# Reordering a fused attention and SwiGLU kernel on one core: scores two units at a time, rest products bank by bank, single steps unsplit

## The chip, the cores and the metric

The kernel runs on one core of one Trainium2 chip. Its engines run side by side, each through its own instructions in the order in which the kernel issues them: PE (TensorE, matmuls and weight loads), ACT (ScalarE), DVE (VectorE), POOL (GpSimd) and SP, which here only starts transfers. The metric is the device time of one execution in microseconds (us); less is better. Three runs of the kernel before gave 430.53, 430.70 and 430.71 us, so the median is 430.70 us.

## The reference

The inputs q, k, v have shape 8 x 12 x 448 x 64 (batch, head, sequence, head dimension). What is computed is attention, and then a SwiGLU block on its output as 3584 tokens of 768 values, with 1536 hidden values:

```
scores = (q @ k.T) / sqrt(64)
attn   = softmax(scores)
x      = (attn @ v), heads side by side     # 3584 x 768
g      = x @ w_gate
out    = ((g / (1 + exp(-g))) * (x @ w_val)) @ w_out
```

## The kernel before

**Units and pairs.** Two heads make a pair; there are 48 pairs, six per batch. Pairs 0 to 11 cut the 448 keys into four chunks of 112. One pair and one chunk is a unit. From pair 12 on (QUAD) a pair has three chunks of 128 keys, and the 64 keys left over, its rest, share one tile with the rest of the neighbouring pair.

For a unit, `qk` (lines 353 to 367; `qk_quad`, lines 324 to 351, from pair 12) does one score matmul per head on PE, into one tile of the pool `ps_s`, and one exponential of both heads on ACT. The score matmuls contract over 64 rows, one head on each half of the array. `ps_s` has three tiles of two banks each, handed out in turn: whoever takes a tile waits until the tile three places earlier has been read. `ps_f` has two tiles of one bank.

The product with the values follows later. In batch 0 it is `pv_chunk` (lines 377 to 411, called a piece here): eight matmuls into the pair's `ps_f` bank, and at the pair's fourth chunk a reciprocal and a multiplication on DVE. `copy_v` (line 216) brings the values into place on DVE; `prep(pr)` gives `turn` (lines 293 to 303), 18 transposes of queries and keys on PE into a tile of `ps_s`, with a copy on DVE; `turn_x` (lines 475 to 493) turns a finished pair on PE, three matmuls, and copies it on DVE into X, which the SwiGLU block reads.

From pair 12 on the product is `pv_open` (two banks, one per head), `pv_rest` (lines 439 to 442: for each of four query blocks j, for each head hx, one matmul with the 64 leftover keys; the two heads use different halves of the array's rows and different banks), `pv_pieces` (24 matmuls on full rows) and `pv_close` (DVE).

**The first stage.** Batch 0 runs ahead of the SwiGLU work. The loop at lines 1129 to 1151 goes through 24 units, one at a time: the unit's scores, then what stands behind it (a turn, loads, a value copy at the units in CAT, a `turn_x` at those in XAT, zero to two pieces). What is left of the pieces follows in the main loop's first visit (lines 1219 to 1223), after the scores of two more units and `turn_x(4)`. Then the first SwiGLU step begins; its `late` call is `turn_x(5)`, in the middle of its gate product.

**The main loop.** `plan` pairs score chunks with value products, two or three units a visit. Each visit's amount of SwiGLU work is written out in FIRST_STEPS and VISITS (lines 977 to 986). A Step (lines 546 to 624) is a gate product (six matmuls, 384 or 512 wide), a tanh on ACT, a value product and two DVE operations (lines 610 and 616). A split step does its value product in two halves, each closed by itself on DVE: the first half into the spare bank of the gate's `ps_s` tile, the second into a `ps_f` bank. `run_pair` splits the second of its steps; `run_single` (lines 1043 to 1049) is used where a visit has one step. In the trace it occurs three times, at 268.2, 279.3 and 290.4 us, each with 384 columns. In the last part the SwiGLU products are done in another form (Unit, `out_group`), which the change does not touch.

The order is the program's: every engine takes its instructions in the order of these calls.

Of the kernel before, what the change touches and what calls it, by code (L numbers as in the profile page):

```python
# [23 lines left out]
FIRST = 6  # L24
# [40 lines left out]
def kernel(  # L65
# [15 lines left out]
    NC = S // P  # L81
# [9 lines left out]
    KR = MQ // 128  # L91
# [68 lines left out]
    def dummy(n, w=4):  # L160
        wp = ps_f.tile([128, 512], FP32, tag="f", name="wp")
        for _ in range(n):
            nc.tensor.matmul(wp[:, 0 : w * 128], lhsT=warm[:], rhs=warm4[:, 0:w], start=True, stop=True)
# [52 lines left out]
    def copy_v(pr):  # L216
        m = 128 if pr >= QUAD else P
        nc.vector.tensor_copy(Vts[pr % NV][0:m, :, :, 0:D], vraw[0:m, pr % VS])
# [105 lines left out]
    def qk_quad(pr, c):  # L324
        s = ps_s.tile([128, 2, 512], FP32, tag="s", name="s")
        if c < KR:
            t = qkT[pr]
            for hx in range(2):
                nc.tensor.matmul(  # L329
                    s[:, hx, 0:S],  # L330
                    lhsT=t[ts(hx, 64), ts(c + low(pr, hx), 128)],
                    rhs=t[ts(hx, 64), ds(NC * 128, S)],
                    start=True,
                    stop=True,
                )
        else:
            for hx in range(2):
                for p in (pr, pr + 1):
                    lo = low(p, hx)
                    t = qkT[p]  # L340
                    nc.tensor.matmul(  # L341
                        s[ts(1 - lo, 64), hx, 0:S],
                        lhsT=t[ts(hx, 64), ds(0 if lo else KR * 128 + 64, 64)],
                        rhs=t[ts(hx, 64), ds(NC * 128, S)],
                        start=True,
                        stop=True,
                    )
        e = e_new(pr, c)
        nc.scalar.activation(  # L349
            e[:, 0 : 2 * S].rearrange("p (h q) -> p h q", h=2), s[:, :, 0:S], AF.Exp, scale=sm_scale  # L350
        )

    def qk(pr, c):
        if pr >= QUAD:
            return qk_quad(pr, c)
        t = qkT[pr]
        s = ps_s.tile([128, 2, 512], FP32, tag="s")
        for hx in range(2):
            nc.tensor.matmul(  # L359
                s[:, hx, 0:S],  # L360
                lhsT=t[ts(hx, 64), c * P : c * P + 128],
                rhs=t[ts(hx, 64), ds(S + (1 - hx) * D, S)],
                start=True,
                stop=True,
            )
        e = Es[pr % NE][:, ds(c * EB, 16)].rearrange("p (h b) x -> p h (b x)", h=2)
        nc.scalar.activation(e[:, :, 0:S], s[0:P, :, 0:S], AF.Exp, scale=sm_scale)  # L367
# [9 lines left out]
    def pv_chunk(pr, c):  # L377
        if c == 0:
            accs[pr] = ps_f.tile([128, 512], FP32, tag="f", name="acc")
        e = Es[pr % NE]  # L380
        vo = Vts[pr % NV][0:P]
        a7 = accs[pr][:, 0 : 7 * (D + 1)].rearrange("p (s d) -> p s d", s=7)
        for j in range(3):
            for hx in range(2):
                nc.tensor.matmul(  # L385
                    a7[:, 2 * j + hx],
                    lhsT=e[:, ds(c * EB + 9 * hx + 2 * j, 2)].rearrange("p b x -> p (b x)"),
                    rhs=vo[:, hx, c, 0 : D + 1],
                    start=c + j + hx == 0,
                    stop=False,  # L390
                )
        for hx in range(2):
            nc.tensor.matmul(
                a7[:, 6],
                lhsT=e[:, ds(c * EB + 6 + hx, 2)].rearrange("p b x -> p (b x)"),
                rhs=vo[:, hx, c, 0 : D + 1],
                start=False,
                stop=c == NC - 1 and hx == 1,
            )
        if c < NC - 1:  # L400
            return
        r = attp.tile([128, 8], FP32, tag="R8", bufs=2, name="R")
        xt = Xts[pr % NX]
        nc.vector.reciprocal(r[:, 0:7], a7[:, :, D])
        n = 7
        nc.vector.tensor_tensor(
            xt[:, 0:n],
            a7[:, 0:n, 0:D],
            r[:, 0:n].unsqueeze(2).to_broadcast([128, n, D]),
            ALU.mult,  # L410
        )

    def pv_mm(pr, hx, c, j, acc, first, last):
        lo = low(pr, hx)
        if c < KR:
            rows, e, col = slice(0, 128), eslot[pr, c][0], c + lo
        else:
            rows, col = (slice(0, 64), 0) if lo else (slice(64, 128), KR)
            e = eslot[pr - pr % 2, RU][0]
        nc.tensor.matmul(  # L420
            acc[:, ts(j, D + 1)],
            lhsT=e[rows, ds(hx * S + j * 128, 128)],
            rhs=Vts[pr % NV][rows, hx, col, 0 : D + 1],
            start=first,
            stop=last,
        )
# [10 lines left out]
            pv_mm(pr, hx, c, j, accs[pr][hx], False, c == KR - 1 and j == KR)  # L437

    def pv_rest(pr):
        for j in range(KR + 1):  # L440
            for hx in range(2):
                pv_mm(pr, hx, RU, j, accs[pr][hx], j == 0, False)

    def pv_close(pr, hx):
# [30 lines left out]
    def turn_x(pr):  # L475
        b, hp = divmod(pr, NHP)
        kk, bb = divmod(b, NB)
        if kk not in X:
            X[kk] = xp.tile([128, NCB, NB * S], FP16, tag="X", name="X")
        dst = X[kk][:, hp, ts(bb, S)]  # L480
        xt = Xts[pr % NX]
        if pr < XPE:
            tp = accs[pr] if pr < FIRST else ps_f.tile([128, 512], FP32, tag="f", name="xtp")
            for j in range(3):
                nc.tensor.matmul(
                    tp[:, ts(j, 128)],
                    lhsT=xt[:, 2 * j : 2 * j + 2].rearrange("p h d -> p (h d)"),
                    rhs=ident[:],
                    start=True,
                    stop=True,  # L490
                )
            nc.vector.tensor_copy(dst[:, 0:MQ], tp[:, 0:MQ])
            return
        nc.sync.dma_start_transpose(
            dst[:, 0:MQ].rearrange("p (j q) -> p j q", j=KR),
            xt[:, 0 : 2 * KR].rearrange("p j d -> p (j d)"),
        )
        nc.sync.dma_start_transpose(
            dst[:, MQ:S].rearrange("p (j q) -> p j q", j=1),
            xt[0:D, 2 * KR : 2 * KR + 2].rearrange("p h d -> p (h d)"),  # L500
        )
# [18 lines left out]
    gate_small = [False]  # L520
# [363 lines left out]
    with tc.manual_schedule():  # L884
# [33 lines left out]
        def emit(item):  # L918
            if item[0] == "qk":
                load_qk16(*item[1:])  # L920
            elif item[0] == "V":
                load_v(item[1] * GP, GP)
            else:
                load_w(*item)
# [86 lines left out]
        def add_sum(n=1):  # L1011
            for _ in range(n):
                if sums:
                    sums.pop(0)()
# [27 lines left out]

        def run_single():
            step = fvq.pop(0)
            step.split = step.alone = not gate_small[0]
            step.gate()
            step.value(0)
            step.finish()
            add_sum()
# [69 lines left out]
        def share(total, at, n):  # L1119
            return (at + 1) * total // n - at * total // n  # L1120

        XAT = (10, 14, 17, 21)
        CAT = (3, 7, 9, 13, 17, 21)
        pieces = [(p, c) for p in range(FIRST) for c in range(NC)]

        def piece():
            pv_chunk(*pieces.pop(0))

        for u in range(FIRST * NC):
            pr, c = divmod(u, NC)  # L1130
            qk(pr, c)
            if u == 1:
                dummy(1)
                turn()
                dummy(1)
            elif u == 3:
                dummy(2)
            elif u == 4:
                prep(2)()
            elif u >= 6 and c == 2:  # L1140
                prep(pr + 2)()
            if c == 1:
                for w in wq.pop(pr, []):
                    emit(w)
            if u in CAT:
                copy_v(CAT.index(u))
            if u in XAT:
                turn_x(XAT.index(u))
            for _ in range(2 if c == 3 else int(c != 2 or u > 12)):
                if u >= 4 and pieces[0][0] * NC + pieces[0][1] <= u - 3:  # L1150
                    piece()

        queue = []
        units = [divmod(x, NC) for x in range(QUAD * NC)]
# [11 lines left out]
        while g < last or queue:  # L1166
            n = 2 if g < WIDE * NC else 3
# [33 lines left out]
        for x, (chunks, todo) in enumerate(plan):  # L1201
# [15 lines left out]
                turn_rests(0)  # L1217
            end = min([y for y in adds if y > x] + [len(plan) + 1])
            if x == 0:
                turn_x(4)  # L1220
                while pieces:
                    piece()
                add_block(0, end)
            early = [p0 for p0 in vcopies.get(x, []) if p0 < QUAD or x > base]
# [31 lines left out]
            if 0 < base - x <= len(FIRST_STEPS):  # L1256
                n = FIRST_STEPS[x - base]
# [141 lines left out]
        first, behind = (pair[0][1] for pair in groups5)  # L1399
# [22 lines left out]
        for m, fn in enumerate(final[0][0][1]):  # L1422
            u = NFB - 1 if m else NH - 1
# [35 lines left out]
```

## Time and profile before

| what | value |
| --- | --- |
| median of three runs | 430.70 us |
| the profiled execution | 430.92 us |
| its span from first to last instruction | 429.1 us |
| around the span | 1.8 us |
| PE busy | 421.0 us, 98% |
| DVE, ACT, POOL busy | 271.0, 245.4, 232.7 us |
| mean granted TensorE clock | 0.996 |

All times in the text count from the start of the span. In a timeline, neighbouring instructions of one line are merged: a row gives the start, the length from the first start to the last end, and how many there are ("x8"). Matmuls are pipelined: a matmul's own duration is much longer than the distance from its start to the next one's. So PE's work is read from distances between starts. In brackets stands the idle time before a row, and what ended it.

### The profile page before, as it was taken

How to read it: one execution, taken by the hardware profiler on the slowest of the kernel's cores; microseconds unless marked ns; L12 is line 12 of the kernel's file. 1: busy time of each engine (PE TensorE's matmuls, PEld its weight loads, DVE VectorE, ACT ScalarE, POOL GpSimd, SP SyncE). 2: the span in 40 equal slices, each digit the busy share in tenths (PEclk: the TensorE clock that was granted, in tenths of full speed). 3: DMA queues.
4: the chain of work that ended last, by engine and by line, in shares of the span. 5: the costliest groups of instructions: out<-in, count | busy, mean ns of one | idle time of the engine just before them, and what ended most of it. 6: DMA issues, size and time to landing. Idle time of an engine off the chain costs nothing.

```text
span 429.1 us, 11647 instructions
## 1 busy us (share of the span) xinstructions
PE 421.0 (98%) x4651; PEld 290.7 (68%) x4651; DVE 271.0 (63%) x643; ACT 245.4 (57%) x395; POOL 232.7 (54%) x356
## 2 busy tenths in 40 slices
PE   8999999999999999999999999999999999999995
PEld 3665665655457777757666677777889985555794
DVE  4666562795668565665635786667777765665662
ACT  6975667656656655646666546559654225455221
POOL 8755543998894773567654777915998000000001
PEclk9999999999999999999999999999999999999998
DMA  9999999999999999999899998713101240000134
GB/s 139 180 200 200 200 176 176 134 176 213 149 145 131 126 159 102 161 127 122 113 162 126 148 151 116 131 28 96 23 2 37 76 124 26 0 2 1 38 91 132
DMA packets 107527, 49.77 MB, mean 116 GB/s; under 512 B 59840, under 2 KB 104208, under 8 KB 107472
## 3 DMA queue, kind: packets, MB, share of 16 engines
q0 software_dynamic: 46944, 24.83, 52.5%
q1 hardware_dynamic: 60384, 24.02, 32.3%
q8 instruction: 36, 0.59, 0.6%
q14 instruction: 19, 0.16, 0.1%
q10 hardware_dynamic: 144, 0.17, 0.1%
HBM read 49.55 MB, written 11.01 MB: 141 GB/s over the span
## 4 chain that ended last, share of the span: by engine, by line
PE 90%; DVE 5%; ACT 2%; DMA 1%; issue 1%; SPq 0%; DVEq 0%
PE og L679 18%; PE gp L557 16%; PE vp L557 12%; PE un L795 10%; PE acc L420 8%; PE ub L795 8%; PE s L329 5%; PE op L650 4%; PE acc L385 2%; PE s L359 2%; PE tp L302 1%; PE s L341 1%; DVE t L610 1%; PE op L1003 1%; DVE hts L616 1%; DMA rk<-in_k_dram 1%
## 5 line engine op out<-in xcount | busy, mean ns | idle before, releaser
L349 ACT ACTIVATE E<-s 128x896 f16<-128x896 f32 x126 | 106.6, 918 | 40.5 <-PE s L329 28.5
L557 PE MATMUL gp<-X,wg 128*128 128x384 f16 (+1 forms) x360 | 73.9, 347 | 0.0
L237 POOL COPY qk<-qkraw 128x512 f16<-128x512 f16 x72 | 44.1, 657 | 54.4 <-DMA qkT<-qk 50.4
L557 PE MATMUL vp<-X,wv 128*128 128x384 f16 (+3 forms) x360 | 66.7, 321 | 0.1
L610 DVE SCALAR_TENSOR_TENSOR t<-sg,gp 128x384 f32<-128x384 f32 (+1 forms) x60 | 36.3, 607 | 40.3 <-ACT sg L584 40.1
L557 PEld LDWEIGHTS <-wv 128*128 128x128 f16 x462 | 43.8, 98 | 26.0 <-issue 0.7
L640 POOL DMA_DIRECT2D out_dram<-osb x3 | 1.6, 541 | 90.8 <-ACT osb L698 90.8
L557 PEld LDWEIGHTS <-wg 128*128 128x128 f16 x360 | 32.8, 98 | 26.1 <-issue 1.9
L584 ACT ACTIVATE sg<-gp 128x384 f32<-128x384 f32 (+1 forms) x60 | 32.1, 537 | 29.1 <-PE gp L557 28.4
L177 POOL DMA_DIRECT2D vraw<-in_v_dram x72 | 43.9, 630 | 6.2 <-DVE hts L616 4.5
L177 POOL DMA_DIRECT2D qkraw<-in_k_dram x70 | 42.6, 624 | 8.5 <-DMA wo<-in_moe_w_out_dram 5.6
L367 ACT ACTIVATE E<-s 112x896 f16<-112x896 f32 x48 | 40.5, 919 | 8.4 <-PE s L359 8.1
L420 PEld LDWEIGHTS <-E 128*128 128x128 f16 (+1 forms) x1152 | 37.5, 96 | 10.9 <-issue 4.7
L679 PEld LDWEIGHTS <-hts 128*128 128x128 f16 x528 | 44.1, 98 | 0.3
L420 PE MATMUL acc<-vo,E 128*128 128x65 f16 (+1 forms) x1152 | 42.2, 192 | 0.8 <-DVE hts L616 0.7
L616 DVE SCALAR_TENSOR_TENSOR hts<-t,vp 128x384 f16<-128x384 f32 (+3 forms) x60 | 32.4, 541 | 5.7 <-PE vp L557 1.6
L698 ACT ACTIVATE osb<-og 128x384 f32<-128x384 f32 x22 | 10.8, 492 | 39.4 <-PE og L679 37.5
L200 POOL DMA_DIRECT2D qkraw<-in_q_dram x44 | 30.1, 683 | 5.1 <-DMA wg<-in_moe_w_gate_dram 1.3
L450 DVE TENSOR_TENSOR xt<-acc,R 128x256 f16<-128x256 f32 x72 | 30.6, 425 | 2.5
L329 PE MATMUL s<-qkT 64*128 64x448 f16 x216 | 30.2, 354 | 0.2
L679 PE MATMUL og<-wo,hts 128*128 128x192 f16 x264 | 29.0, 246 | 0.0
L679 PEld LDWEIGHTS <-hsum 128*128 128x128 f16 x300 | 25.5, 98 | 1.0
(179 smaller groups left out, 727.6 us busy)
## 6 DMA issues: line engine op xcount, KB each, us to landing
vraw<-in_v_dram POOLq DMA_DIRECT2D x72, 64.0 KB, 4.8
qkraw<-in_q_dram POOLq DMA_DIRECT2D x41, 112.0 KB, 4.2
qkraw<-in_k_dram POOLq DMA_DIRECT2D x68, 64.0 KB, 4.7
wg<-in_moe_w_gate_dram POOLq DMA_DIRECT2D x8, 288.0 KB, 10.0
wv<-in_moe_w_val_dram POOLq DMA_DIRECT2D x8, 288.0 KB, 10.1
wo<-in_moe_w_out_dram POOLq DMA_DIRECT2D x2, 1152.0 KB, 17.4
out_dram<-osb SPq DMA_DIRECT2D x7, 288.0 KB, 3.8
out_dram<-osb SPq DMA_DIRECT2D x6, 336.0 KB, 3.2
```

The source lines that it names most:

```text
L177: eng.dma_start(dst[ts(s, 64)], rows)
L237: nc.gpsimd.tensor_copy(dst.rearrange("p c h d -> p h c d"), src)
L329: nc.tensor.matmul(s[:, hx, 0:S], lhsT=t[ts(hx, 64), ts(c + low(pr, hx), 128)], rhs=t[ts(hx, 64), ds(NC * 128, S)], start=True, stop=True,)
L349: nc.scalar.activation(e[:, 0 : 2 * S].rearrange("p (h q) -> p h q", h=2), s[:, :, 0:S], AF.Exp, scale=sm_scale)
L367: nc.scalar.activation(e[:, :, 0:S], s[0:P, :, 0:S], AF.Exp, scale=sm_scale)
L420: nc.tensor.matmul(acc[:, ts(j, D + 1)], lhsT=e[rows, ds(hx * S + j * 128, 128)], rhs=Vts[pr % NV][rows, hx, col, 0 : D + 1], start=first, ...
L557: nc.tensor.matmul(dst[:, 0:w], lhsT=wslice(kind, self.fb, cb), rhs=X[kk][:, cb, ds(c0 + lo, w)], start=(cb == 0), stop=(cb == NCB - 1),)
L584: self.readers = [nc.scalar.activation(self.sg[:, 0:n], gp[:, 0:n], AF.Tanh, scale=0.5)]
L610: nc.vector.scalar_tensor_tensor(self.t1[:, 0:n], self.sg[:, 0:n], 1.0, self.gp[:, 0:n], ALU.add, ALU.mult)
L616: nc.vector.scalar_tensor_tensor(self.hts[:, self.fb, ds(lo, w)], self.t1[:, ds(lo, w)], 0.5 * HS, vp[:, 0:w], ALU.mult, ALU.mult)
L679: nc.tensor.matmul(dst, lhsT=lhs(n), rhs=rhs(n), start=first and n == 0, stop=n == NH - 1, skip_group_check=True)
L795: mm = nc.tensor.matmul(dst, lhsT=lhs[:, n], rhs=rhs[:, n], start=first and n == 0, stop=n == NK - 1, skip_group_check=True,)
```

## The change

Four edits, all of order:

1. The first stage takes two units at a time: the scores of both, then what stands behind the first, then what stands behind the second. XAT and CAT change, the number of pieces behind a unit goes by its chunk alone (1, 2, 0, 1), and `turn_x` comes after the pieces instead of before them.
2. `turn_x(4)` moves from ahead of the leftover pieces to ahead of the last two.
3. `pv_rest` has head outside and query block inside: four matmuls into one bank, then four into the other.
4. `run_single` does not split its step.

```diff
     def pv_rest(pr):
-        for j in range(KR + 1):
-            for hx in range(2):
+        for hx in range(2):
+            for j in range(KR + 1):
                 pv_mm(pr, hx, RU, j, accs[pr][hx], j == 0, False)
...
             step = fvq.pop(0)
-            step.split = step.alone = not gate_small[0]
             step.gate()
...
-        XAT = (10, 14, 17, 21)
-        CAT = (3, 7, 9, 13, 17, 21)
+        XAT = (9, 13, 17, 21)
+        CAT = (3, 7, 11, 15, 19, 23)
...
-        for u in range(FIRST * NC):
+        def behind(u):
             pr, c = divmod(u, NC)
-            qk(pr, c)
...
             if u in CAT:
                 copy_v(CAT.index(u))
+            for _ in range((1, 2, 0, 1)[c]):
+                if u >= 4 and pieces[0][0] * NC + pieces[0][1] <= u - 3:
+                    piece()
             if u in XAT:
                 turn_x(XAT.index(u))
-            for _ in range(2 if c == 3 else int(c != 2 or u > 12)):
-                if u >= 4 and pieces[0][0] * NC + pieces[0][1] <= u - 3:
-                    piece()
+
+        for u in range(0, FIRST * NC, 2):
+            for n in (u, u + 1):
+                qk(*divmod(n, NC))
+            for n in (u, u + 1):
+                behind(n)
...
             if x == 0:
-                turn_x(4)
                 while pieces:
+                    if len(pieces) == 2:
+                        turn_x(4)
                     piece()
```

With sN for the scores of unit N, pN for the piece of unit N, tN for the turn of pair N and xN for `turn_x(N)`, PE's order from unit 12 on was

```
s12 p8 s13 p9 s14 t5 x1 p10 s15 p11 p12 s16 p13 s17 x2 p14 s18 t6 p15 s19 p16 s20 p17
s21 x3 p18 s22 t7 p19 s23 p20 s24 s25 x4 p21 p22 p23
```

and becomes

```
s12 s13 p8 p9 p10 x1 s14 s15 t5 p11 s16 s17 p12 p13 p14 x2 s18 s19 t6 p15 s20 s21
p16 p17 p18 x3 s22 s23 t7 p19 s24 s25 p20 p21 x4 p22 p23
```

## The prediction

> **What bounds the kernel now.** First the busy line of the page, then the timelines of PE and ACT in the first stage, then a stretch of the main loop.
>
> ```profile
> PE 421.0 (98%) x4651; PEld 290.7 (68%) x4651; DVE 271.0 (63%) x643; ACT 245.4 (57%) x395; POOL 232.7 (54%) x356
> ```
>
> PE has hardly any idle time, so PE time that is added or saved shows in the end, unless a wait behind it takes it up. PE in the first stage:
>
> ```profile
> 22.57 0.36 PE L359 MATMUL s<-qkT 64*128 64x448 f16 x2
> 22.86 0.35 PE L385 MATMUL acc<-vo,E 112*128 112x65 f16 x6
> 23.05 0.23 PE L393 MATMUL acc<-vo,E 112*128 112x65 f16 x2
> 23.21 0.36 PE L359 MATMUL s<-qkT 64*128 64x448 f16 x2
> ...
> 26.52 0.55 PE L359 MATMUL s<-qkT 64*128 64x448 f16 x4
> 27.12 0.34 PE L485 MATMUL acc<-ident,xt 128*128 128x128 f16 x3
> 27.30 0.34 PE L385 MATMUL acc<-vo,E 112*128 112x65 f16 x6
> 27.48 0.22 PE L393 MATMUL acc<-vo,E 112*128 112x65 f16 x2
> 27.54 0.34 PE L385 MATMUL acc<-vo,E 112*128 112x65 f16 x6
> ```
>
> Scores to piece takes 0.29 us and piece to scores 0.35; but the two scores at 26.52 stand 0.55 - 0.36 = 0.19 apart, and piece to piece (27.30 to 27.54) takes 0.24. So each change between the half-array scores and other matmuls costs PE 0.10 or 0.11 us. ACT there:
>
> ```profile
> 6.55 13.50 ACT L367 ACTIVATE E<-s 112x896 f16<-112x896 f32 x16 [0.50 <-PE s L359]
> 20.37 8.50 ACT L367 ACTIVATE E<-s 112x896 f16<-112x896 f32 x10 [0.32 <-PE s L359]
> ...
> 32.97 1.73 ACT L367 ACTIVATE E<-s 112x896 f16<-112x896 f32 x2 [0.84 <-PE s L359]
> ```
>
> An exponential lasts 0.92 us, and two in a row start 1.73 - 0.92 = 0.81 apart. The 26 end at 28.87; at 0.81 each they would end at 6.55 + 25 x 0.81 + 0.92 = 27.72. ACT is nearly a bound too. In the main loop, the rests:
>
> ```profile
> 266.55 0.55 PE L329 MATMUL s<-qkT 64*128 64x448 f16 x4
> 266.94 0.28 PE L420 MATMUL acc<-vo,E 64*128 64x65 f16 x8
> 267.13 0.36 PE L329 MATMUL s<-qkT 64*128 64x448 f16 x2
> 267.43 0.91 PE L420 MATMUL acc<-vo,E 128*128 128x65 f16 x24
> ```
>
> Eight rest matmuls start within 0.28 - 0.19 = 0.09 us (one lasts 0.19): pairs, one per head, start 3 ns apart and run side by side. The 24 full-row matmuls of the same width start (0.91 - 0.19) / 23 = 31 ns apart.
>
> **Part 1, two units at a time.** Ten pairs of scores become neighbours (s24 and s25 already are), each saving one change into scores and one out: 10 x 0.21 = 2.1 us of PE. But scores and turns share three tiles. In s9 p4 p5 p6 x0 s10 s11 t4 p7 s12 s13 the tile of s13 is that of s11, so s13 waits for exponential 11. From s9 on:
>
> - s9 to s10: scores to piece 0.29, three pieces 0.72, `turn_x` to scores 0.27 (14.91 to 15.18): 1.28.
> - s10 to exponential 10: 0.41 (6.15 to 6.55 at the first). Exponential 11 starts 0.81 later and lasts 0.92.
> - Its end to s13: 0.05 (before, s3 at 8.33 after an exponential that ended at 8.28).
>
> That is 3.47 us for four units, and the same chain leads from s13 to s17, s21 and s25. PE's own work in a cycle is 1.28 + 0.19 + 0.29 + 0.57 (turn to piece, 21.65 to 22.22) + 0.35 + 0.19 = 2.87, so PE stands 0.6 us ahead of each such score, and behind it, in order, stand all later pieces. Before, s9 was at 13.40 and s25 at 26.72: 3.33 per four units. The 2.1 us saved turn into waiting.
>
> Start of the cycle: t2 now waits for exponential 3, which ends at 9.97, and starts at 10.02; three pieces follow: 10.02 + 0.57 + 0.48 + 0.35 = 11.42 for s6; exponentials 6 and 7 start at 11.83 and 12.64, the latter ends at 13.56, so s9 is at 13.61. Then s25 is at 13.61 + 4 x 3.47 = 27.49.
>
> Behind s25 stand four pieces, not three: p20 at 27.78, p21 28.02, x4 28.26, p22 28.44, p23 28.68. From p23 to `turn_x(5)` it was 27.78 to 29.14, 1.36 us (reciprocal, multiplication); so it is at 30.04 instead of 29.14. **Part 1: +0.9 us.** From there the gate product goes on as before.
>
> What costs nothing here: the value copies, 0.28 us of DVE each, come two to four units later, but end before PE, held at the tile, reaches their piece; without that cover one would cost up to 0.3. POOL's loads keep their order and are passed by nothing; their waits are for earlier landings. SP issues nothing new. **Part 2:** `turn_x(4)` costs PE the same; its 0.56 us copy (28.6 to 29.2) must end before the gate product's fifth matmul (28.9 + 4 x 0.16 = 29.6), and does.
>
> **Part 3, bank by bank.** Four matmuls of one head use the same rows, and so can't run side by side. By the nearest row, 30 ns each: seven distances of together 6 x 30 + 3 = 183 instead of 95 ns, **+0.085 us** a rest. There are 36. In nine the trace has PE waiting at the second matmul, for the second bank (at 112.79 by 0.64 us): there one head's four now go before the wait, and 3 x 30 ns follow it where 88 ns did: 0. In six a third score follows which waited 0.07 us for DVE, over which the added time goes: 0.015 each. The other 21 pay in full: 21 x 0.085 + 6 x 0.015 = **+1.9 us**. Bounds: 36 x 0.09 = 3.2 if nothing hides; below, -0.4, if PE started a matmul every 13 ns (95 / 7) in either order, when the nine would end 3 x 16 ns sooner. I take 1.9, since in full-row pieces equal rows give 31 ns.
>
> [...]
>
> **Part 4, singles whole.** Three times. Value in halves: 12 x 82 ns; whole: 6 x 162; equal. The third score after it waited for the first half's closing (DVE end 270.87, score 270.93); the gate's tile is now free at the end of line 610, 270.49, so that score is 0.19 us earlier (0.3 at the last). What is late next is the second bank of the rests: its closing, 0.55 us whole against two of 0.35, ends at 271.05 to 271.15, where it was 271.14. Part 4: 0 to -0.1 each; I take -0.05 in all. Bounds: -0.7 if all score waits were gain, +0.6 if a closing came 0.2 later.
>
> **Sum** against the profiled execution: 430.92 + 0.9 + 1.9 - 0.05 = 433.7. It stands 0.22 above the median of the runs, so **433.4 us** on their scale. A measurement of this kernel can tell about 0.2%, 0.86 us.
>
> **Rivals.**
>
> - *Exponentials set the pace.* If ACT never starves, exponential 23 ends at 6.55 + 23 x 0.81 + 0.92 = 26.10, s25 is at 26.15 and `turn_x(5)` at 26.15 + 1.19 + 1.36 = 28.70: -0.45 in part 1, 432.1 in all. For it: before, ACT was starved for just 1.15 us. Against: the cycle worked out.
> - *The rests are taken up.* Exponentials' pace, and waits of later scores take half or more of part 3: 430.7 - 0.45 + 0.5 to 0.9 = 430.7 to 431.2, no change. Against: between 125 and 290 us PE's waits are rarely over 0.1.
> - *The changes of the array decide* (other side). Part 1 gives PE its 2.1 us, if a score's tile is free when PE comes back, which needs 0.6 us less in each cycle. With the rests at 1.9 that is 430.5, no change; with the rests under 1.2 it is faster, at half price 429.5. For it: PE is at 98%, and the changes are plain in the rows. Against: the three tiles.
> [...]
>
> Chances: forecast 0.62, exponentials' pace 0.12, taken up 0.14, changes of the array 0.10, weight loads 0.02. Slower 0.62 + 0.12 + 0.02 = 0.76, no change 0.14, faster 0.10. The range, 430.9 to 434.8, takes in the rests at 3.2 and most of the second rival, and leaves out the last two.
>
> **What would show it.** In the first stage PE idle about 0.6 us before s9, s13, s17, s21 and s25, an exponential waited for; s25 near 27.5, `turn_x(5)` near 30.0. Rests without a wait in 0.37 us instead of 0.28; the six scores behind rests without their wait. In the singles the third score no longer waiting for line 616, and the rests' second bank still free at the same distance from line 610. Wrong: s25 before 26.7, or rests that still take 0.28.

## The result and the profile after

The changed kernel took 431.84 us in the median of 11 runs (431.35 to 433.36), the kernel before 430.60 beside it. The ratio is 1.0028, with a 95% interval of 1.0018 to 1.0039: **+1.2 us, 0.8 to 1.7.** Forecast was slower by 2.7 us. The sign was right; the forecast size was over double the measured one. The profiled execution took 432.17 us, its span 430.4.

The busy line of the page after:

```profile
PE 420.6 (98%) x4633; PEld 290.0 (67%) x4633; DVE 267.7 (62%) x640; ACT 245.6 (57%) x395; POOL 232.0 (54%) x356
```

It tells nearly nothing: the share is the same 98%. PE's timeline in the first stage tells more. Here is one cycle, from the wait for s13 to that for s17:

```profile
16.48 0.36 PE L359 MATMUL s<-qkT 64*128 64x448 f16 x2
17.27 0.36 PE L359 MATMUL s<-qkT 64*128 64x448 f16 x2 [0.42 <-ACT E L367]
17.57 0.35 PE L385 MATMUL acc<-vo,E 112*128 112x65 f16 x6
...
18.30 0.33 PE L485 MATMUL acc<-ident,xt 128*128 128x128 f16 x3
18.57 0.55 PE L359 MATMUL s<-qkT 64*128 64x448 f16 x4
19.05 0.63 PE L302 MATMUL tp<-ident,qkraw 112*64 112x112 f16 x18
...
19.96 0.36 PE L359 MATMUL s<-qkT 64*128 64x448 f16 x2
20.75 0.36 PE L359 MATMUL s<-qkT 64*128 64x448 f16 x2 [0.42 <-ACT E L367]
```

The pair s12 s13 is not side by side, as s14 s15 at 18.57 are: between its halves PE waits until an exponential frees the tile. The bracket says 0.42 us, since a matmul's own duration, 0.36 us here, counts as busy; by the starts it is 16.48 to 17.27, 0.79 where 0.19 would do, so 0.6 us are lost. The cycle takes 20.75 - 17.27 = 3.48 us. The wait view of 6 to 31 us has it five times, where before the only wait of a score for an exponential was 0.13 us at s3. (Ahead of the first of the five, a turn at 10.21 us waits 0.40 us for an exponential, too.)

```profile
PE s L359 <- ACT E L367: 2.2, 5, 0.4
```

ACT shows the other side. Before, two rows held all 26 exponentials; now the row breaks where the first score of every other pair comes clearly late, and 22.51 to 26.05 is a cycle of 3.54 us for four exponentials that alone, starting 0.81 apart, take 3.24:

```profile
12.01 10.30 ACT L367 ACTIVATE E<-s 112x896 f16<-112x896 f32 x12 [0.24 <-PE s L359]
22.51 3.34 ACT L367 ACTIVATE E<-s 112x896 f16<-112x896 f32 x4 [0.20 <-PE s L359]
26.05 3.34 ACT L367 ACTIVATE E<-s 112x896 f16<-112x896 f32 x4 [0.20 <-PE s L359]
```

The last scores stand at 27.83 instead of 26.72, and `turn_x(5)`, in the middle of the first gate product, at 30.39 instead of 29.14, **1.25 us later**. By the first score, which itself starts at 6.15 us before and at 6.06 after, the late turn comes after 22.99 and 24.34 us: 1.35 later.

In the main loop, the visit of which the prediction showed the rests, and the single step that follows it:

```profile
268.30 0.30 PE L420 MATMUL acc<-vo,E 64*128 64x65 f16 x8
268.50 0.36 PE L329 MATMUL s<-qkT 64*128 64x448 f16 x2
268.80 0.91 PE L420 MATMUL acc<-vo,E 128*128 128x65 f16 x24
...
270.51 1.14 PE L557 MATMUL vp<-X,wv 128*128 128x384 f16 x6
...
271.30 0.56 DVE L610 SCALAR_TENSOR_TENSOR t<-sg,gp 128x384 f32<-128x384 f32 x1 [0.73 <-ACT sg L584]
...
271.95 0.55 DVE L616 SCALAR_TENSOR_TENSOR hts<-t,vp 128x384 f16<-128x384 f32 x1
```

The eight rest matmuls take 0.30 us in this order, not the 0.37 that I had worked out; before it was 0.28. The score at 268.50 follows 0.20 us behind the rests' first start, as it did before (266.94 to 267.13): the added time went into its wait. The single step behind them is now closed by one operation, from 271.95 to 272.50, and the rests' second bank is taken at 272.56.

Along the way the shift against before is 1.25 us at the first rest (78.94 against 77.69), 1.10 at the third, 1.39 at the last (301.28 against 299.89), and 1.28 at the end. So the first stage makes the loss, and the rests add 0.3 us. The 0.15 that goes between the first and the third rest lies in a visit in which DVE is busy nearly throughout (7.15 of the 7.46 us from 84.93 to 92.39); in the profile of `e3_single` below, in which nothing before 268 us was changed, 0.19 goes there as well, so it varies from execution to execution.

### The profile page after: what moved, and what is told of

It reads as the page before. It is cut to its first block, busy times and chain, and to the rows that moved or that the text cites. A ratio compares the mean times of both kernels' runs of the same rounds, so it can differ in the third digit from the quotient of the medians.

```text
span 430.4 us, 11608 instructions
## 1 busy us (share of the span) xinstructions
PE 420.6 (98%) x4633; PEld 290.0 (67%) x4633; DVE 267.7 (62%) x640; ACT 245.6 (57%) x395; POOL 232.0 (54%) x356
## 4 chain that ended last, share of the span: by engine, by line
PE 93%; ACT 3%; DVE 2%; issue 1%; DVEq 0%; ACTq 0%
PE og L679 18%; PE gp L557 17%; PE vp L557 13%; PE un L795 10%; PE acc L420 8%; PE ub L795 8%; PE s L329 6%; PE op L650 5%; ACT E L367 2%; PE acc L385 2%; PE s L359 2%; PE s L341 1%; PE wp L163 1%; PE op L1003 1%; PE tp L302 1%
## 5 line engine op out<-in xcount | busy, mean ns | idle before, releaser
L557 PE MATMUL vp<-X,wv 128*128 128x384 f16 (+3 forms) x360 | 68.2, 325 | 0.1
L557 PEld LDWEIGHTS <-wv 128*128 128x128 f16 x444 | 42.4, 98 | 26.7 <-issue 0.5
L420 PEld LDWEIGHTS <-E 128*128 128x128 f16 (+1 forms) x1152 | 39.0, 96 | 10.6 <-issue 3.0
L420 PE MATMUL acc<-vo,E 128*128 128x65 f16 (+1 forms) x1152 | 43.6, 193 | 0.6 <-DVE hts L616 0.3
```

Source lines behind the costliest of these rows:

```text
L420: nc.tensor.matmul(acc[:, ts(j, D + 1)], lhsT=e[rows, ds(hx * S + j * 128, 128)], rhs=Vts[pr % NV][rows, hx, col, 0 : D + 1], start=first, ...
L557: nc.tensor.matmul(dst[:, 0:w], lhsT=wslice(kind, self.fb, cb), rhs=X[kk][:, cb, ds(c0 + lo, w)], start=(cb == 0), stop=(cb == NCB - 1),)
```

## The experiments

The theories: **A**, the three score tiles make the loss, and rests cost little; **B**, the rests cost what I predicted; **C**, the first stage loses by the work left behind its last scores, not by its cycle; **D**, matmuls on different halves of the array's rows do not wait for each other; **E**, all matmuls start in the program's order.

### One part at a time

Three kernels, each the kernel before with one part of the change. Parts 1 and 2, `e1_pairs`: all the edits in the first stage and nothing else.

> Parts 1 and 2 alone on the kernel before. Theory A (the three score tiles hold the second score of every other pair, and that is nearly the whole loss): +1.1 to +1.3 us over before, the gate product's late turn near 30.4 us, PE idle 0.42 us before five scores. Rival B (the rests cost what I predicted, 1.9 us, and the first stage 0.9): +0.9 us.

Measured: ratio 1.0023 (1.0014 to 1.0032), +1.0 us; late turn at 30.25, which is 24.43 us behind the first score, and five waits as in the changed kernel.

Part 3 alone, `e2_rests`:

```diff
-        for j in range(KR + 1):
-            for hx in range(2):
+        for hx in range(2):
+            for j in range(KR + 1):
```

> Part 3 alone on the kernel before. Theory A: rests without a wait start their eight matmuls within 0.11 us instead of 0.095, so +0.3 to +0.4 us in all. Rival B: 0.18 us each, +1.9 us in all.

Measured: ratio 1.0000 (0.9992 to 1.0009), so between -0.3 and +0.4 us. 1.9 us would be 1.0044: B falls. In its trace the shift against before grows by 0.28 us from the third rest to the last, as in the changed kernel, while in `e1_pairs`, with the rests as before, it stays at 0.87 to 0.86. The runs can't tell 0.28 us from nothing.

Part 4 alone, `e3_single`:

```diff
-            step.split = step.alone = not gate_small[0]
```

> Part 4 alone on the kernel before. Both theories: the third score behind each of three steps starts 0.2 to 0.3 us earlier, the second bank of the rests comes free when it did; 0 to -0.1 us. A rival in which the score's wait is the price: -0.6 us.

Measured: ratio 0.9998 (0.9990 to 1.0007). The waits moved as expected: in each of the three places the score's wait for line 616 is gone and the rests' second matmul starts 0.27, 0.28 and 0.40 us behind the first, where it was 0.06: it waits for the second bank. The three parts measured alone, 1.0, 0.0 and -0.1 us, make up the 1.2 us of the whole within their intervals.

### The cycle made shorter and longer

`e4_even` is the changed kernel with one piece behind every unit:

```diff
-            for _ in range((1, 2, 0, 1)[c]):
+            for _ in range(1):
```

> The changed kernel with one piece behind every unit, instead of 1, 2, 0, 1 by chunk. The pairs and the four pieces behind the last scores stay. Theory A: from the second score of a pair to the first of the next it is one piece less, 1.04 us, so a cycle of four units takes 3.23 instead of 3.47 us; the last scores stand near 27.0 instead of 27.8, the late turn near 29.7 instead of 30.4; -0.6 to -0.8 us against the changed kernel. Rival C (the loss is in the work left behind the last scores, whatever the cycle): no change from the changed kernel, late turn at 30.4.

Measured: 430.83 us, ratio 1.0006 to before (0.9998 to 1.0014), so 0.9 us less than the changed kernel by the two ratios. The late turn is at 29.03, 23.19 us behind the first score (24.34 in the changed kernel), though four pieces still stand behind the last scores: C falls. The cycles took 3.29, 3.33, 3.39 and 3.39 us, not 3.23; now the turn too waits for its tile, 0.07 to 0.17 us in each cycle.

`e10_longer` goes the other way:

```diff
-            for _ in range((1, 2, 0, 1)[c]):
+            for _ in range((2, 2, 0, 0)[c]):
```

> The changed kernel with 2, 2, 0, 0 pieces behind a unit by chunk, instead of 1, 2, 0, 1: from unit 12 on, one piece more between the second score of a pair and the first of the next, and five pieces instead of four behind the last scores. Theory A: three cycles of four units take 0.24 us more each, 3.72 instead of 3.48; with the fifth piece behind the last scores the late turn comes 0.9 to 1.0 us later than in the changed kernel: +0.9 us against it, +2.1 against before. Rival C (only the work left behind the last scores counts): +0.24 us against the changed kernel.

Measured: ratio 1.0103 (1.0089 to 1.0117), +4.4 us against before and 3.2 to 3.3 against the changed kernel. The direction is A's, but the size is over three times the 0.9 us expected: I had overlooked something. Its PE timeline:

```profile
17.52 0.36 PE L359 MATMUL s<-qkT 64*128 64x448 f16 x2 [0.44 <-ACT E L367]
17.81 0.35 PE L385 MATMUL acc<-vo,E 112*128 112x65 f16 x6
...
18.55 0.34 PE L385 MATMUL acc<-vo,E 112*128 112x65 f16 x6
18.73 0.22 PE L393 MATMUL acc<-vo,E 112*128 112x65 f16 x2
19.18 0.34 PE L485 MATMUL acc<-ident,xt 128*128 128x128 f16 x3 [0.23 <-DVE xt L406]
19.46 0.55 PE L359 MATMUL s<-qkT 64*128 64x448 f16 x4
...
21.64 0.36 PE L359 MATMUL s<-qkT 64*128 64x448 f16 x2 [0.44 <-ACT E L367]
```

There are four pieces between 17.52 and 19.18, and the first of them is now the last of a pair, whose DVE work the turn behind them needs: by the starts the turn comes at 19.18 instead of 18.79. So the stretch from the second score to the next pair grew from 1.30 (17.27 to 18.57) to 1.94 us, by 0.64, and the cycle from 3.48 to 4.12, by the same 0.64. That is A's chain: whatever stands in that stretch, work or waiting, lengthens every cycle. Four such cycles make 2.6 us, the work behind the last scores 0.9 (a fifth piece and a longer wait of the turn), and s9 stands 0.4 earlier: 3.1 us to the late turn.

### Turns moved without pairs, and pairs that lose nothing

`e7_units_turned` is the kernel before, unit by unit, with the moved `turn_x` alone:

```diff
-        XAT = (10, 14, 17, 21)
+        XAT = (9, 13, 17, 21)
...
-                turn_x(4)
                 while pieces:
+                    if len(pieces) == 2:
+                        turn_x(4)
                     piece()
```

> The kernel before, one unit at a time, with only two things of the change: the first two turns of finished pairs one unit earlier, and the fifth ahead of the last two pieces. Theory A (the pairing is the loss): 0 to -0.3 us against before. Rival C (the moved turns are the loss): +0.5 us or more.

Measured: ratio 1.0011 (0.9990 to 1.0031), too wide to tell 0.3 us. From the first score to the late turn its profile has 23.00 us, before 22.99: the moved turns lose nothing. But the equality hides two waits:

```profile
9.10 0.63 PE L302 MATMUL tp<-ident,qkraw 112*64 112x112 f16 x18
10.03 0.34 PE L385 MATMUL acc<-vo,E 112*128 112x65 f16 x6 [0.30 <-DVE vo L218]
```

Here PE waits for a value copy whose transfer landed later than in the kernel before, where PE did not wait for it. And in the kernel before the piece at 19.57 waited 0.13 us for the copy of `turn_x(1)`; in the profiles of `e2_rests` and `e3_single`, whose first stage is that of before, it waited 0.67 and 0.37. With the turns moved this wait is gone. So they may bring 0.1 us or more, which no run here tells, and the first stage of one and the same kernel takes 22.99 to 23.56 us from execution to execution.

`e8_pairs_late` was to keep the pairs and lose nothing. Against the changed kernel:

```diff
-            for _ in range((1, 2, 0, 1)[c]):
+            for _ in range((1 + (u in (7, 23))) if u >= 7 else int(c != 2)):
...
-        for u in range(0, FIRST * NC, 2):
+        for u in [0, *range(2, 8), *range(8, FIRST * NC, 2)]:
+            these = (u, u + 1) if u == 0 or u >= 8 else (u,)
```

> A version meant to keep the pairs and lose nothing: single units up to unit 7, pairs from unit 8, one piece behind every unit and a second one behind units 7 and 23, so that three pieces and not four are left behind the last scores; rests and single steps as before. By the cycle worked out (3.24 us for four units, set by the exponentials): the last scores near 26.4, the late turn near 28.8, -0.3 us against before. If the pairs lose for another reason than the tile: +0.5 us or more.

Measured: ratio 1.0006 (0.9992 to 1.0019); the last scores at 27.01 instead of 26.4, the late turn at 29.32 instead of 28.8. The waits of the second scores fell from 0.42 to 0.10 and 0.18 us, but another wait came, as PE's timeline shows:

```profile
25.70 0.34 PE L385 MATMUL acc<-vo,E 112*128 112x65 f16 x6
25.88 0.22 PE L393 MATMUL acc<-vo,E 112*128 112x65 f16 x2
26.46 0.36 PE L385 MATMUL acc<-vo,E 112*128 112x65 f16 x6 [0.36 <-DVE vo L218]
```

With a piece of the sixth pair moved ahead of the last scores, that pair's value copy, which CAT now puts at unit 23, is late: on DVE it stands behind the copy of a turn (25.55 to 26.21).

`e9_pairs_late_copies` is that version with the copies back to where they were:

```diff
-        CAT = (3, 7, 11, 15, 19, 23)
+        CAT = (3, 7, 9, 13, 17, 21)
```

> The version with pairs from unit 8 again, with the value copies where they were before the change (units 9, 13, 17, 21 instead of 11, 15, 19, 23). In the last try PE waited 0.36 us at 26.46 for the sixth pair's value copy, issued at unit 23 just ahead of its piece. Theory A: that wait goes, the last scores stand near 26.4 to 26.6, the late turn near 28.8; -0.2 to -0.4 us against before, which this measurement may not tell from no change. If the pairs lose for another reason: +0.5 us.

Measured: 430.44 us, ratio 0.9996 (0.9987 to 1.0005): no change that can be told. The wait is gone, the last scores stand at 26.67 and the late turn at 29.02, 23.21 us behind the first score. In this order pairs cost nothing that can be told, but they bring nothing either: PE still waits seven times for a tile, 0.10 to 0.37 us each.

### How the rest matmuls start

Why do eight matmuls, four of one head and then four of the other, start within 0.11 us? Two kernels do each rest twice, the first result being overwritten. `e6_twice_alt` alternates the heads; `e5_twice_bank` takes one head's eight and then the other's:

```diff
+        for hx in range(2):
+            for again in range(2):
+                for j in range(KR + 1):
+                    pv_mm(pr, hx, RU, j, accs[pr][hx], j == 0, j == KR and not again)
```

> The kernel before, with each rest product done twice, bank by bank: eight matmuls of one head, then eight of the other; the first four of each are overwritten by the second four. Theory D (matmuls of the two halves of the array's rows do not wait for each other; a head's later matmuls are overtaken by the other head's): sixteen matmuls start within about 0.24 us. Rival E (starts in order; equal rows 30 ns apart): 14 x 30 + 3 ns, 0.42 us. Between the two if PE looks only a few matmuls ahead.

> The same sixteen matmuls, heads alternating. Both theories: eight pairs, 30 ns apart, 0.21 to 0.23 us. The difference to the doubled product bank by bank is the price of the order alone.

Measured: ratios 1.0160 (1.0123 to 1.0197) and 1.0073 (1.0046 to 1.0099); 437.81 and 434.03 us, 3.8 us apart. The same rest with the 24 pieces behind it, first bank by bank, then alternating:

```profile
130.28 1.38 PE L420 MATMUL acc<-vo,E 64*128 64x65 f16 x40
```

```profile
130.14 1.24 PE L420 MATMUL acc<-vo,E 64*128 64x65 f16 x40
```

The difference is 0.14 us, and 27 rests without a wait make 27 x 0.14 = 3.8. The sixteen starts span 0.22 us alternating, and bank by bank 0.356: neither the 0.24 of free halves (D) nor the 0.42 of starts in order (E), but between, which the expectation of the first had for a PE that looks a few matmuls ahead. The starts bank by bank are, in ns from the first:

```
0 29 64 93 122 131 151 170 181 205 216 234 263 292 321 356
```

By spacing these split into two rows with some 30 ns between neighbours: 0 29 64 93 122 151 181 216 and 131 170 205 234 263 292 321 356. So the second head's first starts 9 ns behind the first head's fifth, ahead of the three that come before it in the program. In the changed kernel the eight starts are 0 8 29 46 64 81 93 110, that is 0 29 64 93 and 8 46 81 110: again three are overtaken. Only where the second bank is not free do the four of one head stand alone; this is the changed kernel at the rest where PE waited longest:

```profile
113.94 0.28 PE L420 MATMUL acc<-vo,E 64*128 64x65 f16 x4
114.56 0.63 PE L420 MATMUL acc<-vo,E 64*128 64x65 f16 x12 [0.34 <-DVE hts L616]
```

Four take 0.28 us there; eight took 0.30 above. So the sentence ahead of the prediction, that every engine takes its instructions in the order of the calls, does not hold for the starts of these matmuls: by the spacing, three of a rest's eight start ahead of earlier ones on the other half of the rows. One thing more in the traces bears the split out: they keep, with each matmul, the semaphore that it waits for. Behind the first matmul of a rest only the one that opens the second bank has anything to wait for; at 113.94 us it is the fifth to start, as in the program, and the semaphore is DVE's. In 17 of the changed kernel's 27 rests without a wait a mark stands on the second matmul to start, 8 to 17 ns behind the first, and in the other ten on none behind the first. In `e5_twice_bank` it stands, in 20 rests, on the sixth to start, 125 to 131 ns behind the first, where the program has this matmul ninth.

## Why the prediction was wrong

**Part 1, +0.9 us: right in mechanism, somewhat too small.** The profiles have +1.25 at the late turn and 1.10 at the third rest, the runs of the part alone +1.0 (0.6 to 1.4). The cycle was forecast at 3.47 and took 3.48 twice and 3.54 twice, the last two because the exponential followed its score by 0.46 instead of 0.41 us. Another 0.18 came ahead of the cycle: s9 at 13.79 instead of 13.61. In this profile the first exponential started 0.1 us later than before, 0.60 us behind its score instead of 0.41; `e6_twice_alt`, whose first stage is that of before, has 0.60 too, so this is not the change's. With what the first stage of one kernel varies by itself, the size of part 1 is known to some 0.3 us. All five waits stand where they were forecast, and from s25 to the late turn it was 2.57 us, forecast 2.55.

**Part 2 and what was put at nothing: right** for the changed kernel. The later value copies do no harm there; the sixth pair's owes that to its piece standing behind the last scores, and `e8_pairs_late` shows this cover gone, at 0.36 us.

**Part 3, +1.9 us: this step failed.** It reads "Four matmuls of one head use the same rows, and so can't run side by side. By the nearest row, 30 ns each: seven distances of together 6 x 30 + 3 = 183 instead of 95 ns". The 30 ns within a head are right. Wrong was that the other head's four would wait for them: their first starts 8 ns after the first of the first head. The seven distances sum to 110 ns, so a clean rest costs 0.015 us and not 0.085. 21 x 0.015 = 0.3 us, and 0.3 is what the profile has. The six rests with a waiting score, forecast at 0.015 each, and the nine with a wait for the bank cost nothing that shows. With 0.3 in place of 1.9 the sum of the prediction's own terms would have been 430.7 + 0.9 + 0.3 - 0.05 = 431.85. That this hits the 431.84 so closely is luck: part 1 is not known that well.

**Part 4, -0.05: right in mechanism.** The wait moved from the score to the second bank, and the shift against before is 1.37 us ahead of the three singles and 1.37 to 1.38 behind them. The runs cannot tell -0.05 from nothing.

**The rivals.** Exponentials' pace did not come. Its sum, 432.1, is nearer to the measured time than the forecast, but by luck: it had -0.45 for part 1 and 1.9 for part 3. Nor did the changes of the array decide: `e9_pairs_late_copies` has the pairs without the waits of 0.42 us, and gains at most 0.6 us by its interval; shorter waits for tiles remain in it. That weight loads hold up the matmuls of one head, put at 0.02 among the chances and, like the changes of the array, left out of the range, no run shows: in the changed kernel a head's four alone, at 113.94 us, start 29 to 34 ns apart, each with a load of 92 to 95 ns. The rival of the rests being taken up, with 0.5 to 0.9 us for part 3, comes nearer to the 0.3 than the forecast, but for the wrong reason: no later wait takes them up, they start sooner.

**What stays open.** That the second head's first matmul is ahead of its place stands in the traces; which head the matmuls behind it belong to is inferred from spacing. What lets them start early was not tried, nor whether more than three can be overtaken.

## What to carry to other kernels

Two pieces of work that share a short ring of buffers can save their changeover by standing side by side only if the buffer of the second is free by then: follow the ring back to what frees it, and add what stands between that pair and the next, as it lengthens every round (in `e10_longer` 0.64 us more of it made each cycle 0.64 us longer). A busy share of 98% hid 0.6 us of waiting per round here; starts showed it. And before an order of issue is priced as an order of execution, look for a place where the same instructions stand alone beside one where they don't.

## What the runs showed of the hardware

- Matmuls on one half of the array's rows started ahead of up to three earlier ones on the other half: by the spacing, in the changed kernel's rests without a wait (starts 0 8 29 46 64 81 93 110 ns) and in the rests of sixteen of `e5_twice_bank`, whose ninth matmul in the program was the sixth to start, 131 ns behind the first. On the same rows they kept some 30 ns for 65 columns: 29 to 34 where four stand alone (113.94 us of the changed kernel), 29 to 39 by the split above.
- A change between half-array scores and pieces cost PE about 0.1 us each way, in both kernels: score to piece 0.29 to 0.30 us and piece to score 0.34 to 0.35, against 0.20 from score to score and 0.24 to 0.26 from piece to piece (first stage, before and changed).
